# Attention and gated experts on one core: the first batch's q and k stacked on two sides of the array and turned by 64x128 transposes

## The chip, the cores and the metric

The kernel runs on one core of a Trainium2 chip. The metric is the device time of one execution in microseconds (us). The engines, as the profile names them: PE (TensorE, matrix products), PEld (its weight loads), DVE (VectorE), ACT (ScalarE), POOL (GpSimd) and SP (SyncE, which issues DMA transfers and computes nothing). Each engine works through its own list of instructions in order. Matrix products land in PSUM, eight banks of 128 x 512 words, and have to be copied out by DVE or ACT.

## What is computed

```python
B, H, S, D = 8, 8, 576, 64          # q, k, v: (B, H, S, D), float32
scores = q @ k^T / sqrt(D)
# heads 0-3: local mask, 0 <= row - col < 32
# heads 4-7: strided mask, row >= col and row % 32 == col % 32
x = softmax(masked scores) @ v       # heads side by side: (B, S, 512)

logits = x @ w_gate                  # 4 experts, the top 2 kept, softmax over these
for e in range(4):
    a = softmax(causal((x @ wq[e]) @ (x @ wk[e])^T / sqrt(64)))
    out += w_e * (a @ (x @ wv[e]) @ wo[e])
```

## The kernel before, in words

The kernel runs through eight batches. `stage1(b, hp)` does the first attention for a pair of heads (four pairs a batch: pairs 0 and 1 are local, 2 and 3 strided). It loads q and k, turns them so that the head dimension lies on partitions, forms the few scores that the mask leaves, does the softmax in six steps, multiplies by V and splits the result into a high and a low part, `xh` and `xl`, which later matmuls use three at a time to keep precision. `project` forms q and k of the experts, `values2` V and the gate, `last_scores` and `attend` the second attention, `out_tile` the output.

For batches 1 to 7 q and k are loaded in blocks and turned by VectorE (`turn`, L494). For batch 0 (`whole`) they are loaded in long rows and turned on TensorE: `tps` multiplies 64x64 blocks by an identity (L462, 200 matmuls in four quarters of the array), and `tp_out` copies each PSUM bank into the tile `qkt` (the copies stand under L304, the line of a helper). A local pair's q goes to one tile `nat` and its k to another, with both heads on partitions (128 rows of 2304 B); a strided pair's are 36 rows of 4096 B for each head. They rest in tiles that other things use later (`vs`, and `p`, the P2 rings). Scores are L535 (local) and L542 (strided), values L634 and L657, the transposes of strided softmax results L605, projections of batch 0 L794, V projections L711 and L719 (the short last tile).

V of batch 0 and 1 goes through three tiles `VR` (`load_v`, L505 local, L512 strided; two DMAs a step, one for each head), weights through `load_weights` (L388, L391). All loads are issued by SyncE.

The order is written out: `PLAN` is a list of words such as `242S0`, each an operation's number, the engine that does it and the buffer slots it takes, and `schedule` issues them in that order. An operation that is queued on an engine waits there for its data, and what stands behind it waits too. `fill` (L1022) is a matmul of ones that nobody reads; the plan places 60 of them where TensorE would stand idle.

A DMA from SyncE or ScalarE is counted on one of eight counters, and a DMA waits for the last one on its counter. In the listings below `DMAHW3` is such a counter, and `[waits DMAHW3_49]` a wait for it.

Of the kernel before, what the change touches and what calls it, by code (L numbers as in the profile page):

```python
# [20 lines left out]
def attention_moe_kernel(  # L21
# [69 lines left out]
    def op(kind, eng, n, key, fn, r=(), w=(), mode=None, npk=0, after=()):  # L91
# [24 lines left out]
        242S0 43P0 230S1 17P1 60S0 44P2 151S0 29P3 7P4 99S1 38P5 61S2 28P6 243A0 110S1 12P7 231A0 21P0 236S2 232G0  # L116
        47P1 141S0 30P2 139S1 244G0 15P3 26P4 100S3 24P5 11P6 182S0 32P7 3P0 109S 62P10 101P21 140S 237A 63D 71S2
        64P3 238G 102A 27P4 65D 66P5 183S1 184S 23P6 67A 4P7 68P0 1P1 303S4 69A 6P2 155S 16P4 74P360 152S 76D 148P70
        138S 75D 239S 78D0 13P5 149A 181S 77D 80G 37P1 34P2 144P0 79G 82A 227S3 84D 81A 103P4 245S 145D 107P6 73S
        83D 104A 10P3 108D 240A 35P5 270S0 14P1 85D 241G 20P7 112S 105P2 86G 45P0 228A 106D 8P3 271S 87G 41P4 246A  # L120
        229D 46P5 70S 247D 113P611 88D0 142P7 114D 115D 72S 146P0 116D1 143A 117D 118G 154S 0P3 147A 31P2 119G 40P4
        120A 251S0 36P5 191P61 122D 121A 123D 156P170 124D 192A 125G 185P3 111S 157D 126G 158D 33P2 334S2 159D2 186A
        39P0 160D 187P4 153S 161G 127D1 162G 163A 89P561700 188D 252A0 164A 253G0 165D 302S 166D 9P2 92A 224S 96A
        2P0 93D 94A 189P3 167D 90A 95D 150S 169G 91D 97D 128P426011 194S2 98G 190A 168G 1260P10 135A 131A 136D 129A
        170P570 132D 225A 137G 195S 130D 199P301 133A 226G 172D 171A 197S 134D 1266P2 193S 200D 173P4722 201D 202D3
        1267P 203D 204G 174A 198S 178A 48P5 175D 25P6 176A 205G 206A 179D 19P3 233S 1246P0 177D 208D 180G 207A 18P5
        272S 1247P 209D 196S 1296P61 210D 1268P 211G 300S 1253P3 266S3 1289P7 212G 1297P 234A 1254P 213P451 235D
        254S1 1261P 215A 214D 1290P 257S 1262P 216P5433 307S1 1291P 248S 221A 217A 1298P 222D 219A 255A 220D 1303P4
        218D 273S 256G 1248P 306S 1304P 258A 223G 267S 1292P 259D 301S 1305P 1294A0 1249P 268S 1293A 249A 1269P
        1295G0 335S 1250A 250D 1263P 269S 1271A1 1251A 275D0 1299P 1264A 260S0 1252G1 1281P50 1270A 1265D 1300A 337S  # L130
        1272D 1301A 341S0 1275P7 308D1 1302G 1282A 338S 304S 336S 1283P0 1255P 1276A 274D 1284A 1318P160 261A0
        1323P250 1320D0 1319D 280P700 1322A 263S1 262G0 1324D 1321A 1325D 305S 1326A 1306P 281D 339S 1327A 1273P6
        282D 312S1 1307A 283D0 340S 1308D 284G 1279P1 477S4 1274A 342D0 264A 276S0 265G 285A 309D 1256P 313S 1309P2
        1280A 286D 1257A 1277P5 1258A 377S3 343D 1259G 372S2 1310P 1278A 287D 42P7 344S2 1285D00000 288G 5P0
        1375P461 474S 1328P131 376S 1349P571 1329D 371S 1286A 1311P 1330D 373S 1331A 22P0 1376D1 346S 1332A 1350D2
        1312P 374S 1313A 1287D 1314A 1378A 311S 1316P1301 1315D 1288G 1352A 1333D 1317P40 1351D 1337G 310S 350P520
        1354D 1338G 1353A 1411D3 370S 1385P710 1335G 352D 375S 1336G 351D 407S1 1355D 1334G 277S 353D1 1339G 1356A
        1340P322 314P541 1387D 476S 354G 1342A 1386D 1341A 411S0 1380P121 1389A 1357D 279S 315D 1343P370 1358G 355A
        1382D 1381D 1360G 1388A 1361P523 356D 1362A 347S 1383A 316D 1359G 1363A 357D 408S 378D0 1345A 358G 1364P151
# [942 lines left out]
```

## Time and profile before

| what | us |
|---|---|
| median of 3 runs | 451.67 |
| lowest and highest run | 451.58, 454.35 |
| the profiled execution | 455.44 |
| its span, first to last instruction | 453.7 |

The page's busy times are for the whole span, and its slices show how an engine's share changes. PE's matmuls are pipelined, so that a busy PE need not be at its peak, and a filler is as busy as a useful matmul. The granted clock is a share of TensorE's 2.4 GHz: 1.00 is 2.4 GHz, 0.50 is 1.2 GHz. A "pass" in what follows is one MATMUL record of the trace; a float32 matmul leaves two, a transpose one.

### The profile page before, as it was taken

To read this page: it belongs to the slowest core of one execution; us is meant where nothing else is said; L and a number is where in the kernel's file an instruction comes from. 1 tells how busy PE (TensorE), PEld (TensorE's weight loads), DVE (VectorE), ACT (ScalarE), POOL (GpSimd) and SP (SyncE) were. 2 spreads that over 40 slices of the span, in tenths; PEclk is the share of its full clock that TensorE was granted. 3 is DMA by queue.
4 is the path that set the end of the run, shared out by engine and by line. 5 is a ranking of instruction groups with operands and counts; after the bars stand their busy time and mean duration, and the time that the engine had idled before them with its cause. 6 is when DMAs were issued, how large, how long until landed. Compare 5 with 4: busy or idle time off the path is not lost.

```text
span 453.7 us, 19338 instructions
## 1 busy us (share of the span) xinstructions
PE 436.0 (96%) x7878; PEld 385.8 (85%) x7878; DVE 338.5 (75%) x1037; ACT 270.6 (60%) x835; POOL 224.7 (50%) x352
## 2 busy tenths in 40 slices
PE   8899996899999999999999999999999999999995
PEld 8799995689978988789879997899889998898874
DVE  5257489997799799878789799877998297733650
ACT  2235457863776575734677474845984475755762
POOL 7145456834277715746255616581777017450550
PEclk9789999999999999999999999999999999999999
DMA  6642665555655553644553364335363330200113
GB/s 173 162 92 56 126 115 104 103 104 95 105 97 91 98 125 73 133 88 88 112 119 67 70 129 89 64 67 143 71 148 88 79 84 21 77 1 23 48 49 116
DMA packets 189817, 41.91 MB, mean 92 GB/s; under 512 B 184064, under 2 KB 184064, under 8 KB 189728
## 3 DMA queue, kind: packets, MB, share of 16 engines
q1 hardware_dynamic: 189728, 40.67, 42.7%
q8 instruction: 62, 1.02, 0.9%
q14 instruction: 27, 0.22, 0.2%
HBM read 31.20 MB, written 9.44 MB: 90 GB/s over the span
## 4 chain that ended last, share of the span: by engine, by line
PE 72%; DVE 12%; POOL 7%; issue 3%; DMA 3%; SPq 1%; ACT 1%; DVEq 0%; POOLq 0%; ACTq 0%
PE bank L783 17%; PE bank L1003 9%; PE bank L711 9%; PE bank L974 6%; PE bank L882 5%; PE bank L941 5%; POOL p L922 4%; PE bank L634 3%; PE bank L657 3%; PE bank L462 3%; PE bank L794 3%; PE bank L1022 2%; PE bank L535 2%; DVE p L889 2%; PE bank L719 2%
## 5 line engine op out<-in xcount | busy, mean ns | idle before, releaser
L922 POOL TENSOR_SCALAR p<-p,st,wt 128x256 f32<-128x256 f32 (+3 forms) x128 | 76.2, 608 | 17.6 <-DVE st L902 8.4
L894 ACT ACTIVATE p<-p,st 128x256 f32<-128x256 f32 (+3 forms) x128 | 71.4, 564 | 4.1 <-DVE st L889 3.7
L889 DVE CUSTOM_DVE_ANT_0 p<-bank,m_cau 128x256 f32<-128x256 f32 (+3 forms) x128 | 56.4, 483 | 6.2 <-PE bank L882 5.6
L494 DVE STREAM_TRANSPOSE qkt<-nat 128x576 f32<-128x576 f32 x56 | 55.7, 1006 | 5.0 <-DMA nat<-in_k_dram 4.7
L974 PE MATMUL bank<-th,vs 128*64 128x192 f32 (+4 forms) x512 | 48.0, 337 | 0.5 <-ACT th L304 0.5
L304 ACT COPY th<-bank 128x256 f32<-128x256 f32 (+2 forms) x112 | 43.2, 429 | 8.1 <-PE bank L941 7.3
L974 PEld LDWEIGHTS bank<-th,vs 128*64 128x64 f32 x512 | 33.6, 137 | 13.5 <-issue 5.9
L941 PE MATMUL bank<-ident,p 64*128 64x64 f32 x800 | 39.6, 227 | 5.7 <-POOL p L922 4.6
L941 PEld LDWEIGHTS bank<-ident,p 64*128 64x128 f32 x800 | 33.3, 138 | 13.6 <-POOL p L922 6.9
L812 POOL TENSOR_TENSOR qkl<-kf,qk 128x288 fp32r<-128x288 f32 x32 | 25.8, 806 | 35.2 <-ACT qk L803 30.2
L803 ACT CAST qk<-bank 128x288 fp32r<-128x288 f32 x64 | 25.4, 401 | 29.9 <-PE bank L783 29.8
L619 DVE TENSOR_TENSOR xl<-bank,xh 128x160 fp32r<-128x160 f32 (+3 forms) x112 | 31.1, 322 | 10.8 <-ACT xh L617 10.4
L711 PE MATMUL bank<-wh_v,xh 128*128 128x260 f32 x128 | 37.1, 290 | 0.0
L711 PE MATMUL bank<-wh_v,xl 128*128 128x260 f32 x128 | 36.3, 283 | 0.0
L711 PE MATMUL bank<-wl_v,xh 128*128 128x260 f32 x128 | 36.1, 282 | 0.0
L304 DVE COPY th<-bank 128x384 f32<-128x384 f32 (+2 forms) x48 | 23.0, 496 | 15.6 <-PE bank L941 15.3
L617 ACT CAST xh<-bank 128x160 fp32r<-128x160 f32 (+3 forms) x112 | 27.6, 323 | 11.3 <-PE bank L634 6.1
L571 POOL TENSOR_TENSOR p1s<-p1s,st 128x648 f32<-128x648 f32 (+1 forms) x18 | 20.7, 1157 | 27.2 <-DVE st L569 26.0
L783 PE MATMUL bank<-xh,wh_q 128*128 128x288 f32 x112 | 33.8, 301 | 0.0
L783 PE MATMUL bank<-xh,wh_k 128*128 128x288 f32 x112 | 33.3, 297 | 0.0
L783 PE MATMUL bank<-xl,wh_k 128*128 128x288 f32 x112 | 33.0, 294 | 0.0
L783 PE MATMUL bank<-xh,wl_k 128*128 128x288 f32 x112 | 33.0, 294 | 0.0
(158 smaller groups left out, 1274.4 us busy)
## 6 DMA issues: line engine op xcount, KB each, us to landing
out_dram<-ys SPq DMA_DIRECT2D x32, 256.0 KB
nat<-in_q_dram SPq DMA_DIRECT2D x112, 72.0 KB
nat<-in_k_dram SPq DMA_DIRECT2D x112, 72.0 KB
v<-in_v_dram SPq DMA_DIRECT2D x96, 40.0 KB
v<-in_v_dram SPq DMA_DIRECT2D x128, 22.5 KB
v<-in_v_dram SPq DMA_DIRECT2D x64, 27.0 KB
v<-in_v_dram SPq DMA_DIRECT2D x32, 48.0 KB
out_dram<-ys SPq DMA_DIRECT2D x8, 128.0 KB
```

Source lines behind the costliest of these rows:

```text
L304: (nc.scalar.copy if e == "ACT" else nc.vector.tensor_copy)(dst, src)
L494: nc.vector.transpose(dst, src)
L617: op("xh", "A", n_, key, lambda e, s_=s_, x_=x_: nc.scalar.copy(x_(xh.t), s_(xa.t)), r=[xa], w=[xh[u]])
L619: op("xl", "D", n_, key + 0.5, lambda e, s_=s_, x_=x_: nc.vector.tensor_sub(x_(xl.t), s_(xa.t), x_(f(xh.t))), r=[xa, xh[u]], w=[xl[u]])
L711: nc.tensor.matmul(vp.t[:m, :NV], xx.t[:, t0:t0 + m], ww.t[:, kt, :], start=i == 0, stop=i == 11)
L783: nc.tensor.matmul(pj.t[:, :HS], ww.t[:, kt, ep * 128:(ep + 1) * 128], xx.t[:, c], start=i == 0, stop=i == 11)
L889: lambda e, sp=sp, p=p, a=a, nk=nk, ci=ci: nc.vector.tensor_tensor_reduce(out=p.t[:, a, :nk], in0=sp[a].t[:, :nk], in1=m_cau[:, S - nk:], ...
L894: op("exp2", "A", nk, k_ + 1, lambda e, p=p, a=a, ci=ci, nk=nk: nc.scalar.activation(p.t[:, a, :nk], p.t[:, a, :nk], AF.Exp, bias=st.t[:, ...
L922: lambda e, p=p, a=a, ci=ci, t=t, nk=nk: nc.gpsimd.tensor_scalar(p.t[:, a, :nk], p.t[:, a, :nk], st.t[:, 14 + ci + a:15 + ci + a], wt.t[:, ...
L941: nc.tensor.transpose(tp[hf].t[:, 64 * c:64 * c + 64], src, ident[r, r])
L974: nc.tensor.matmul(acc.t[o, c0:c0 + cn], vw, th[a].t[:, s0:s0 + cn], start=j == 0, stop=j == idx[-1], skip_group_check=True)
L1003: nc.tensor.matmul(yp.t[:, :DM], xx.t[:, c0:c0 + 128], ww.t[:, ep, :], start=i == 0, stop=i == 5)
```

## The change

In batch 0, q of a pair now goes to partitions 0 to 63 and k to partitions 64 to 127 of the same tile, the two heads side by side in the free dimension. A 64x128 block (both heads of q, or of k) is turned by one transpose instruction (L468 in the new numbering, from here on), so that there are 100 in place of 200 matmuls. Each load now moves 256 B runs, and there are four loads for a local pair (two before) and eight for a strided one (four before). The loads of pair 2 are issued by ScalarE. The steps of `load_v` for the local pairs of batch 0 may be issued by ScalarE or GpSimd; the plan gives eight DMAs to each. V of batch 1 may not be loaded ahead of batch 0's. The plan is a new one throughout.

```diff
-        nat = [(NAT if local or not whole else (VS, P2[3])[hp % 2]).new(f"nat{x}_{n}") for x in range(2)]
+        if whole:
+            nat = [r.new(f"nat{x}_{n}") for x, r in enumerate([VS] if local else [(P2[3], VS)[hp % 2]] * 2)]
+        else:
+            nat = [NAT.new(f"nat{x}_{n}") for x in range(2)]
...
+            def load(e, z, x, src, h, g0, g1):
+                dma = nc.scalar if e == "ACT" else nc.sync
+                dst = raw(z)[64 * x:64 * x + wd, :128 * (g1 - g0)].rearrange("p (i h d) -> p i h d", h=2, d=D)
+                dma.dma_start(dst[:, :, h], src[b, h0 + h].rearrange("(p i) d -> p i d", i=nb)[:, g0:g1])
+
+            for z in range(len(nat)):
+                g0, g1 = (0, 9) if local else (8 * z, 8 * z + 8)
+                for x, src in enumerate((q, k)):
+                    for h in range(2):
+                        op("load_big", "A" if hp == 2 else "S", wd, hp, lambda e, z=z, x=x, src=src, h=h, g0=g0, g1=g1: load(
+                            e, z, x, src, h, g0, g1), w=[nat[z]], npk=wd)
...
-                            for h in range(2):
-                                r = slice(64 * h, 64 * h + wd)
-                                nc.tensor.matmul(tp.t[64 * h:64 * h + 64, wd * (g - g0):wd * (g - g0) + wd],
-                                                 raw(x)[r, D * g:D * g + D], ident[r, r], start=True, stop=True)
...
+                        for x in range(2):
+                            r = slice(64 * x, 64 * x + wd)
+                            c = 128 * (g if local else g - g0)
+                            nc.tensor.transpose(tp[x].t[:, wd * (g - g0):wd * (g - g0) + wd], raw(z)[r, c:c + 128], ident[r, r])
...
-            op("load_v", "S", 336 if local else 198, (k0 - 25 if b else 4.0 + hp), lambda e, i=i: load_v(e, i), w=[vt],
-               npk=336 if local else 198)
+            o = op("load_v", "AG" if local and not b else "S", 336 if local else 198, (k0 - 25 if b else 4.0 + hp),
+                   lambda e, i=i: load_v(e, i), w=[vt], npk=336 if local else 198, after=FIRST if b == 1 else ())
+            if b == 0:
+                FIRST.append(o)
...
-        242S0 43P0 230S1 17P1 60S0 44P2 151S0 29P3 7P4 99S1 38P5 61S2 28P6 243A0 110S1 12P7 231A0 21P0 236S2 232G0
```

TensorE before, at the start, where the first fillers end (`fz` are fillers, `nat` are q and k of the local pairs, `ident` the identity, `qkt` the turned q and k):

```order
L1022 MATMUL bank_64<-fz 128x128
L462 MATMUL bank_65<-ident,nat_176 64x64 x10
L462 MATMUL bank_66<-ident,nat_177 64x64 x10
L462 MATMUL bank_67<-ident,nat_178 64x64 x10
L1022 MATMUL bank_68<-fz 128x128
L462 MATMUL bank_69<-ident,nat_176 64x64 x8
...
L535 MATMUL bank_67<-qkt_181 32x64
```

TensorE after, at the same place (`vs_174` now holds both q and k of pair 0):

```order
L1031 MATMUL bank_65<-fz 128x128
L468 MATMUL bank_66<-ident,vs_174 128x64
L468 MATMUL bank_67<-ident,vs_174 128x64
L468 MATMUL bank_66<-ident,vs_174 128x64
L468 MATMUL bank_67<-ident,vs_174 128x64
...
L544 MATMUL bank_65<-qkt_181 32x64
```

Before, 17 fillers stand ahead of the first transpose, and q of both local pairs and k of one are turned ahead of the scores; after, 10 fillers, then the 18 transposes of pair 0 alone, 9 fillers, and its scores. Up to the first L719 (L728 after) there are 46 fillers, 200 transposes and 75 projection matmuls before, and 52, 100 and 87 after.

ScalarE before, from its first instruction (`th` holds raw weights, `wh` their high part):

```order
L394 ACT_TABLE_LOAD
L394 CAST wh_q_254<-th_170 128x256 [waits DMAHW0_49]
L394 CAST wh_k_252<-th_171 128x256 [waits DMAHW1_49]
L394 CAST wh_q_254<-th_172 128x256 [waits DMAHW1_49]
L304 COPY qkt_183<-bank_66 128x5x64 [waits DVE_49,PE_49]
L304 COPY qkt_181<-bank_69 128x4x64 [waits DVE_49,PE_49]
```

ScalarE after, at the same place (`p_166` and `p_167` take q and k of pair 2, `v_189` and `v_185` V of the local pairs):

```order
L450 DMA p_166<-in_k_dram 36x8x64
L450 DMA p_167<-in_q_dram 36x8x64
L450 DMA p_167<-in_k_dram 36x8x64 x2
L450 DMA p_167<-in_q_dram 36x8x64 [waits DMAHW0_49]
L450 DMA p_166<-in_q_dram 36x8x64 [waits DMAHW2_49]
L512 DMA v_189<-in_v_dram 32x6x64 [waits DMAHW4_49,DVE_49]
L512 DMA v_189<-in_v_dram 32x6x64 [waits DMAHW6_49]
L512 DMA v_185<-in_v_dram 32x6x64 [waits DMAHW0_49]
L512 DMA v_185<-in_v_dram 32x6x64 [waits DMAHW2_49]
L304 ACT_TABLE_LOAD
L304 COPY qkt_181<-bank_69 128x4x64 [waits PE_49]
L394 CAST wh_q_254<-th_170 128x256 [waits DMAHW3_49]
```

Ten loads have moved ahead of the table load and of the first copy; six more stand behind the next copy.

GpSimd after, behind its masks, before the first step of the softmax (before, no load stands on GpSimd):

```order
L512 DMA v_185<-in_v_dram 32x5x64
L321 AFFINE_SELECT m_str<-m_str 64x54
L512 DMA v_185<-in_v_dram 32x5x64
L321 AFFINE_SELECT m_str<-m_str 64x54
L321 AFFINE_SELECT m_loc<-m_loc 32x64
L512 DMA v_189<-in_v_dram 32x5x64 x4
L512 DMA v_185<-in_v_dram 32x5x64 x2
L580 TENSOR_TENSOR p1l_80<-p1l_80,st_199 128x320 x2
```

Eight loads stand ahead of the subtraction of pair 0 (L580, which was L571).

## Rows read from the trace of the kernel before

**Rows 1.** The page: busy us, share of the span and instructions of each engine

```profile
PE 436.0 (96%) x7878; PEld 385.8 (85%) x7878; DVE 338.5 (75%) x1037; ACT 270.6 (60%) x835; POOL 224.7 (50%) x352
```

**Rows 2.** Busy time by stretch: stretch, length, each engine (instructions), PEclk, DMA share, GB/s

```profile
0.00:6.25 6.25, 4.58 (x21) 4.59 (x22) 4.78 (x36) 2.09 (x3) 4.43 (x16) 1.00 0.47 121
6.25:16.50 10.25, 8.12 (x209) 7.28 (x209) 3.15 (x6) 2.10 (x4) 5.47 (x13) 1.00 0.82 205
16.50:26.70 10.20, 10.20 (x124) 9.45 (x121) 3.00 (x8) 2.82 (x7) 2.32 (x4) 0.50 0.57 131
...
60.00:100.00 40.00, 35.08 (x795) 28.44 (x790) 37.89 (x108) 29.09 (x90) 26.02 (x37) 1.00 0.53 96
```

**Rows 3.** Chain of waits, 0 to 60 us: start, us, what

```profile
9.70 6.22 DMA vs<-in_k_dram
...
19.07 3.82 PE bank L462 x68
22.89 2.00 PE bank L1022 x8
...
27.43 0.90 PE bank L535 x58
28.33 1.99 PE bank L462 x64
30.32 1.09 PE bank L1022 x8
...
35.78 1.08 PE bank L634 x62
...
40.23 0.52 PE bank L605 x12
40.75 0.84 PE bank L542 x44
...
42.18 0.83 PE bank L657 x44
...
44.88 2.77 PE bank L794 x21
...
55.24 1.02 PE bank L719 x8
```

**Rows 4.** Groups by line and shape, the transposes of batch 0: busy us, mean ns

```profile
L462 PE MATMUL bank<-ident,nat 64*64 64x64 f32 x144 | 6.6, 255 | 0.0
...
L462 PE MATMUL bank<-ident,vs 36*64 36x36 f32 x128 | 5.5, 251 | 2.1 <-DMA vs<-in_k_dram 2.1
...
L462 PE MATMUL bank<-ident,p 36*64 36x36 f32 x128 | 4.6, 224 | 0.0
```

**Rows 5.** Instructions of TensorE in order of time, the first: start, us

```profile
1.67 6.23 PE L1022 MATMUL bank<-fz 128*128 128x128 f32 x34 [1.67 <-DVE fz L312]
```

**Rows 6.** Waits of SyncE's queue up to 60 us: us in total, times, longest

```profile
SPq L512 <- PE bank L634: 4.5, 1, 4.5
...
SPq L451 <- DMA vs<-in_q_dram: 0.8, 1, 0.8
SPq L451 <- DMA nat<-in_k_dram: 0.7, 1, 0.7
```

**Rows 7.** Instructions in order of time, start to 27 us

```profile
0.79 1.28 ACT L394 ACT_TABLE_LOAD   x1 [0.79 <-PEq L1066]
0.80 0.45 SPq L388 DMA_DIRECT2D th<-in_moe_wq_dram  x1
...
3.15 0.41 ACT L394 CAST wh_q<-th 128x256 fp32r<-128x256 f32 x1 [1.07 <-DMA th<-in_moe_wq_dram]
...
26.18 1.07 SPq L391 DMA_DIRECT2D p<-in_moe_w_gate_dram  x1
```

**Rows 8.** DMA queue 1 from 6 to 8 and from 20.5 to 22.5 us: packets, MB, share of 16 engines

```profile
q1 hardware_dynamic: 563, 0.60, 94.4%
...
q1 hardware_dynamic: 1727, 0.37, 87.4%
```

More of the change, by code (lines that the diff above doesn't have):

```diff
@@ L270, in attention_moe_kernel @@
+        2579D 2628P422 2599A 2623G 2600A 2648G 2631P173 2630D 2629A 2601P3 2633A 2632D 2634P600 2604A 2602A 2605D
+        2603D 2649P500 2635A 2652P421 2651D 2650A 2636D 2655P71 2654A 2653A 2663P32 2657D 2656A 2666P51 2664A 2665S
+        2658P0 2667A 2668S 2669P20 2659A 2661A 2660D 2662D 2672P62 2670A 2671S 2675P41 2673A 2674S 2676A 2677S
     """
@@ L453, in stage1 @@
-            for g0, g1 in zip(cuts, cuts[1:]):
-                for x in range(2):
-                    tp = RB.new(f"tp{g0}{x}_{n}")
-                    cn = wd * (g1 - g0)
-                    def tps(e, tp=tp, g0=g0, g1=g1, x=x):
-                        for g in range(g0, g1):
-                            for h in range(2):
-                                r = slice(64 * h, 64 * h + wd)
-                                nc.tensor.matmul(tp.t[64 * h:64 * h + 64, wd * (g - g0):wd * (g - g0) + wd],
-                                                 raw(x)[r, D * g:D * g + D], ident[r, r], start=True, stop=True)
-                    def out(e, tp=tp, g0=g0, g1=g1, x=x, cn=cn):
-                        if local:
-                            copy(e, at(qkt.t, 0, 128, x * S + g0, [[1, g1 - g0], [nb, wd]]),
-                                 tp.t[:, :cn].rearrange("p (i t) -> p i t", t=wd))
-                        else:
-                            copy(e, at(qkt.t, 0, 128, x * S + NJ * g0, [[NJ, g1 - g0], [1, NJ], [16 * NJ, 2]]),
-                                 tp.t[:, :cn].rearrange("p (i u a) -> p i u a", u=NJ, a=2))
-                    op("tp", "P", 2 * (g1 - g0), k0 - 14 + 0.1 * g0, tps, r=[nat[x]], w=[tp, qkt[x]], mode=MQ)
-                    op("tp_out", "AD", cn, k0 - 13 + 0.1 * g0, out, r=[tp], w=[qkt[x]])
@@ new lines, in stage1, with raw @@
+            nb, wd, cuts = (9, 64, (0, 5, 9)) if local else (16, 36, (0, 8, 16))
+            def raw(z):
+                return nat[z].t.rearrange("p a c -> p (a c)")
+            def load(e, z, x, src, h, g0, g1):
[8 more added lines that the diff above has]
+                            e, z, x, src, h, g0, g1), w=[nat[z]], npk=wd)
@@ new lines, in stage1, with tps, out @@
+            for g0, g1 in zip(cuts, cuts[1:]):
+                tp = [RB.new(f"tp{g0}{x}_{n}") for x in range(2)]
+                cn = wd * (g1 - g0)
+                z = 0 if local else g0 // 8
+                def tps(e, tp=tp, g0=g0, g1=g1, z=z):
+                    for g in range(g0, g1):
+                        for x in range(2):
+                            r = slice(64 * x, 64 * x + wd)
+                            c = 128 * (g if local else g - g0)
+                            nc.tensor.transpose(tp[x].t[:, wd * (g - g0):wd * (g - g0) + wd], raw(z)[r, c:c + 128], ident[r, r])
+                def out(e, tp=tp, g0=g0, g1=g1, x=0, cn=cn):
+                    if local:
+                        copy(e, at(qkt.t, 0, 128, x * S + g0, [[1, g1 - g0], [nb, wd]]),
+                             tp[x].t[:, :cn].rearrange("p (i t) -> p i t", t=wd))
+                    else:
+                        copy(e, at(qkt.t, 0, 128, x * S + NJ * g0, [[NJ, g1 - g0], [1, NJ], [16 * NJ, 2]]),
+                             tp[x].t[:, :cn].rearrange("p (i u a) -> p i u a", u=NJ, a=2))
+                op("tp", "P", g1 - g0, k0 - 14 + 0.1 * g0, tps, r=[nat[z]], w=[*tp, qkt[0], qkt[1]], mode=MR)
+                for x in range(2):
+                    op("tp_out", "AD", cn, k0 - 13 + 0.1 * g0, lambda e, out=out, x=x: out(e, x=x), r=[tp[x]], w=[qkt[x]])
```

322 lines of the change are left out of this document (155 added, 167 removed).

## The prediction

> **What bounds the kernel now.** I began with the engine totals and the busy time by stretch. TensorE is busy for 436.0 of the 453.7 us span, VectorE for 338.5 [rows 1]. The stretches say that this is not one limit: between 60 and 100 us VectorE is busy for 37.89 of 40 us, and before 26.7 us every engine but TensorE has room, while the granted clock of TensorE goes from 1.00 (2.4 GHz) to 0.50 (1.2 GHz) between 16.5 and 26.7 us [rows 2]. Then I read the chain of waits over the first 60 us [rows 3]. Up to about 56 us it is nearly all TensorE, but much of that is filler matmuls (L1022, of no use to the output) and the transposes of batch 0 (L462). The reader is to see that filler is planned waiting: where it stands in the chain, what really limits is the arrival of q and k, the copies out of PSUM, or the softmax. One real wait for data stands in the chain: 6.22 us from the issue of a k load to its first transpose at about 16 us.
>
> I call the first matmul of L719 (the short last tile of the V projection of batch 0) the mark. Before, it starts at 55.24 us [rows 3]. The change rewrites what comes ahead of the mark; behind it the same instructions run in another order. So I sum TensorE up to the mark.
>
> **Prices at 2.4 GHz, from [rows 3].** A filler is two passes: 8 passes in 1.09 us, 0.136 each. A 64x64 transpose by matmul is also two passes: 64 in 1.99 us, 0.031 each; the 200 of batch 0 are 144 + 128 + 128 = 400 passes [rows 4]. For the new 64x128 transpose the nearest row is L605, also 64 rows by 128 columns: 12 in 0.52 us, 0.043 each, one pass. A block of local scores is 0.90 us, of strided scores 0.84, of local values 1.08, of strided values 0.83; a projection matmul 2.77 / 21 = 0.132.
>
> **Before, up to the mark.** The first fillers end at 1.67 + 6.23 = 7.9 us [rows 5], the last one lapping over the first transpose: 7.8. The other 58 filler passes are 7.9 us, 400 transpose passes 12.4, two blocks of each of the four kinds 7.3, the 24 transposes of L605 1.0, 75 projections 9.9. Sum 46.3 us. The mark is at 55.24, so 8.9 us are not in it: the wait at 16 us, the half clock (below), switches between shapes.
>
> **After, up to the mark.** Ten fillers stand ahead of the first transposes, not 17. At the 6.23 us / 34 of the old ones they end near 5.3 us. The four loads of pair 0 need not be there yet: the first load of the kernel is issued at 0.80 us and used at 3.15 us, 2.35 later [rows 7], the fourth is issued some 1.4 us behind the first, and the 2304 packets of pair 0 share the DMA engines with the 1152 of the first four loads on ScalarE. Small packets cost 0.874 x 2 us x 16 / 1727 = 16.2 ns of one engine [rows 8], so 3456 of them take 3.5 us from about 2.4 us on. I take 6.7 us (5.3 to 7.8). Then 42 fillers, 84 passes, 11.4 us; 100 transposes 4.3 us (from 3.1, the price of the narrow one, to 8.0, two passes at 0.04); the same 7.3 and 1.0; 87 projections 11.5. Sum 42.2 us, against 46.3: 4.1 less. Twelve projections more lie ahead of the mark, 1.6 us that no longer follow. At equal work the start is **5.7 us** shorter, if the 8.9 us outside the sum stay as they are. That is the step on which the forecast rests.
>
> **The loads.** All q and k of batch 0 (2.36 MB) now come as 9216 packets of 256 B: 9216 x 16.2 ns / 16 = 9.3 us of all 16 engines. In a stretch with many long packets they moved 0.60 MB in 2 us at a share of 94.4%, 318 GB/s at a full share [rows 8], 7.4 us for the same bytes. So 1.9 us more of transfer. The DMA share is 0.82 between 6.25 and 16.5 us and 0.47 and 0.57 beside it [rows 2], so most of this is hidden, and it shows only if pair 1 or 2 arrives late. SyncE loses 16 issues of V and 4 of q and k of pair 2 and gains 8 for the other pairs: 12 fewer at 0.45 us [rows 7], 5.4 us earlier for the weights and batch 1. It also waited 4.5 us with V of pair 3 for the values of a local pair [rows 6]; that wait stays, since the buffers are still three, and comes as early as those values do.
>
> **ScalarE, the new wait.** Ten loads now stand ahead of its table load, which was free at 0.79 us, and of its first copies. Each load waits until an earlier one on the same of eight counters has landed; ScalarE uses four of them, so its fifth load waits for its first and its ninth for its fifth. Such waits were 0.7 and 0.8 us on SyncE [rows 6]. Two rounds of 2.35 us from 0.80 on put the ninth at 5.5 us; if the rounds take 3.5 us, since all share the engines, at 7.8. Two issues of 0.45 and 1.28 us of table load follow: the first copy starts between 7.7 and 10 us, the second ends some 1.7 us later with a weight cast between. The scores of pair 0 wait for it: between 9.4 and 11.7 us, while TensorE by the sum is there at 6.7 + 0.8 + 2.4 = 9.9. So 0 to 1.8 us late; I take 1, inside the 8.9. Behind the last four V loads are queued the copies of pair 1 and the first exponentials.
>
> **GpSimd** issues the other eight loads of the local V, ahead of its first subtraction. No row shows a load issued there. Bounds: SyncE's 0.45 us for one and 1.07, its longest single row here [rows 7]; 3.6 to 8.6 us. GpSimd was busy for 4.43 + 5.47 = 9.9 us by 16.5 us [rows 2], some 1.4 of it the subtraction, so it is free at 12 to 17 us, where the softmax of pair 0 wants it near 14. I take the low end, as the same kind of instruction, and keep 3 us for the range. The Trainium skill, "DMA: Bandwidth & Descriptors", section "Latency and other measured facts", gives about 1 us for the first byte on this path, spent on writing descriptors; by it the eight would be 8 us, near the upper end. No run here shows it yet.
>
> **The clock.** In the half-clock stretch 8 filler passes took 2.00 us, not 1.09, and 68 transpose passes 3.82, 0.056 each [rows 3]. TensorE was idle for 2.1 us in the stretch ahead of it [rows 2]. The new order has such a place too, at the first scores. I leave the loss as it was.
>
> **The rest.** The same instructions; batch 0's attention to 100 us is VectorE's. Batch 1 must arrive 5.7 us sooner, and SyncE's 5.4 us allow that. A new order may be worth 2 us either way.
>
> The profiled execution took 455.44 us, its span 453.7 plus 1.74; the median of the runs is 451.67. The sum is a difference, 5.7 us, and I take it from the median: 451.67 - 5.7 = **446.0 us**.
>
> **Rivals.**
> 1. The loss shrinks as well: no wait at 16 us and no half clock. Of the 8.9 us go the 2.1 that TensorE is idle between 6.25 and 16.5 us [rows 2] and 4.8 of the half clock (rival 4): 446.0 - 6.9 = 439.1. For it: fewer loads on SyncE ahead of pair 1. Against it: busier DMA engines.
> 2. The start is bound by arrival and by ScalarE's queue, not by TensorE. Then what the transposes lose is spent waiting, and the mark stays at 55 to 57: **451.7 us**, no change. For it: idle where filler stands, and the waits above. Against it: two queues and 12 fewer issues on SyncE.
> 3. The gain is given back behind the mark. VectorE, at 95% from 60 to 100 us, needs batch 1's data and the scores; if it can't start sooner, also 451.7. Against it: it is fed by the same chain.
> 4. Slower: the clock stays at 1.2 GHz until the first projection. It has risen once the fillers had run for some 4.5 us; the new ones are fewer and a pause follows. Price: 66 filler passes at 0.114 more, 7.5; 100 transposes at 80% more, 3.4; 4.8 us of scores and values likewise, 3.9; sum 14.8, less the 4.8 that a like count gives for the old half-clock stretch (20 filler passes and 100 transpose passes). So 446.0 + 10.0 = 456.0 us, above before if over 5.7 of the 10 come true. It is decided at the end of the first fillers. The Trainium skill, "TensorE: Matmul & The Clock Gate", section "Part 4: PE-mode transpose", says that transpose mode does not count as busy as a matmul does; the change turns 200 matmuls into 100 such transposes, so by it this rival gains. The old rows neither bear it out nor refute it, as the transposes there stand between matmuls.
> 5. The change does what it says: the order shows 100 transposes at the start. Only half of V's loads on other engines are on ScalarE.
>
> **How the numbers follow.** Forecast 0.40, rival 1 0.18, rival 2 0.20, rival 3 0.09, rival 4 0.13. One per cent, 4.5 us, is about what a measurement of this kernel tells from no change. Over 1% faster (below 447.2) are two thirds of the forecast's chance (a spread of 3 us), rival 1 and a little of 2: 0.50. Over 1% slower (above 456.2) is half of rival 4 and a rest for the order behind: 0.12. Within 1%: 0.38. The range runs from rival 1, and 0.6 us below it, to rival 4: 438.5 to 456.0. The forecast alone is 443 to 449.
>
> **What would show it.** Right: the first transpose near 6.5 us, 100 passes of about 0.045 us, first scores at 10 to 12, the mark near 51, and 453.7 - 55.2 - 1.6 = 397 us behind it. Rival 1: the mark below 47 and the clock at 1.00. Rival 2: the mark at 55 with long idle on TensorE. Rival 3: the mark at 51, but over 400 us behind it, with TensorE idle for VectorE. Rival 4: clock 0.50 beyond 26.7 us. Most at risk are the wait for pair 0 and ScalarE's queue.

## The result, and the profile after

The changed kernel took 449.6 us (median of 16 runs, 445.89 to 453.19) where the kernel before took 454.38 (16 runs, 450.42 to 456.54): a ratio of 0.9896, 95% interval 0.9861 to 0.993, which is 4.7 us (3.2 to 6.3). The forecast was 5.7 us. The time itself lies 3.6 us above the 446.0 on record, 2.7 of them because the base does: 451.67 over three runs then, 454.38 over sixteen now. Ratios here and below leave out the executions that stood well above the rest of their kernel, among them the traced ones of E1 (586.51 us, at a mean granted clock of 0.655) and of E4 (456.92, 0.978). The profiled execution took 447.38 us, its span is 445.7, 8.0 below the profiled one of before; the two lie at different places of their spreads.

The page's engine totals of the changed kernel, which answer to [rows 1], show TensorE with 6.7 us less to do and as full as before:

```profile
PE 429.3 (96%) x7582; PEld 379.4 (85%) x7582; DVE 341.1 (77%) x1049; ACT 267.5 (60%) x827; POOL 226.0 (51%) x356
```

Its busy time by stretch, for [rows 2] (the columns are the same):

```profile
0.00:6.25 6.25, 4.57 (x20) 4.34 (x20) 4.78 (x36) 0.00 (x0) 4.42 (x16) 1.00 0.73 161
6.25:16.50 10.25, 8.81 (x149) 8.11 (x149) 4.13 (x10) 3.97 (x7) 7.49 (x17) 1.00 0.94 188
16.50:26.70 10.20, 8.61 (x270) 7.73 (x270) 8.88 (x24) 5.47 (x16) 5.88 (x10) 1.00 0.62 132
26.70:40.00 13.30, 13.26 (x267) 12.22 (x266) 8.70 (x25) 6.36 (x19) 7.71 (x13) 0.87 0.60 121
60.00:100.00 40.00, 35.00 (x808) 28.77 (x814) 35.88 (x107) 26.26 (x83) 24.85 (x37) 0.96 0.50 90
```

The stretch from 16.5 to 26.7 us stood at a clock of 0.50 before and stands at 1.00 now. The 1.00 ahead of it is not to be trusted: where no clock record lies the view prints full speed, and the pace of the fillers below says 1.2 GHz. The DMA share in the second stretch rose from 0.82 to 0.94.

The chain of waits from 0 to 60 us, for [rows 3]:

```profile
2.90 4.66 DMA vs<-in_q_dram
7.69 1.34 PE bank L468 x18
9.03 4.14 PE bank L1031 x18
13.17 1.15 PE bank L544 x68
...
15.02 1.27 PE bank L468 x34
...
17.38 0.62 PE bank L468 x16
...
19.23 3.75 DMA th<-in_moe_wq_dram
...
49.80 0.96 PE bank L728 x8
```

The mark is at 49.80 us in place of 55.24: 5.4 us. By the instructions' own start it is 49.55, against 55.08; these starts are used below. Behind it are 396.1 us, against 398.6. So in this pair of traces the gain stands at the start, as forecast. How it came about there is another matter. Instructions in order of time, changed kernel:

```profile
1.68 4.64 PE L1031 MATMUL bank<-fz 128*128 128x128 f32 x20 [1.68 <-DVE fz L312]
7.69 1.34 PE L468 MATMUL bank<-ident,vs 64*128 64x64 f32 x18 [1.38 <-DMA vs<-in_q_dram]
8.35 1.28 ACT L304 ACT_TABLE_LOAD   x1 [8.35 <-DMA v<-in_v_dram]
8.96 4.21 PE L1031 MATMUL bank<-fz 128*128 128x128 f32 x18
9.64 0.61 ACT L304 COPY qkt<-bank 128x256 f32<-128x256 f32 x1
10.09 3.42 POOL L512 DMA_DIRECT2D v<-in_v_dram  x6
10.36 0.74 ACT L304 COPY qkt<-bank 128x320 f32<-128x320 f32 x1
13.10 1.22 PE L544 MATMUL bank<-qkt 64*32 64x64 f32 x72
15.02 0.46 PE L468 MATMUL bank<-ident,vs 64*128 64x64 f32 x8
15.84 0.72 POOL L580 TENSOR_TENSOR p1l<-p1l,st 128x320 f32<-128x320 f32 x1 [2.34 <-DVE st L578]
```

And the same place before:

```profile
12.87 0.97 PE L535 MATMUL bank<-qkt 64*32 64x64 f32 x72
15.97 1.31 PE L462 MATMUL bank<-ident,vs 36*64 36x36 f32 x28 [2.12 <-DMA vs<-in_k_dram]
```

The reader is to see two things. First, the scores of pair 0 end at 14.3 us now and ended at 13.8 before, though TensorE had less to do by then. By the prediction's prices it had 46 filler passes, 92 transpose passes and the scores before, 10.0 us, and has 38, 18 and the scores now, 6.8. These 3.2 us are spent: the first transposes wait 1.38 us for q, and 18 filler passes take 4.21 us, 0.23 each, where 2.4 GHz would make them 2.45. Second, all of the lead is won behind that point: 41.2 us from the end of these scores to the mark before, 35.2 now. Of the 6.0 us, 2.0 are work (46 filler and 308 transpose passes before; 66, 82 and twelve more projections now). The other 4.0, by subtraction, are the pause of 2.12 us and the half clock behind it, less what the new order has of both. The two stretches, before and changed, tell these apart:

```profile
13.84:55.08 41.24, 39.12 (x871) 36.38 (x870) 22.11 (x58) 15.90 (x46) 16.07 (x26) 0.88 0.50 102
14.32:49.55 35.23, 33.35 (x675) 30.61 (x676) 24.75 (x63) 17.70 (x53) 16.18 (x25) 0.95 0.63 126
```

TensorE idles for 2.1 us of the one and for 1.9 of the other: the pause is gone, but several small ones have come. The clock takes 0.12 x 41.2 = 4.9 us of the one and 0.05 x 35.2 = 1.8 of the other, some 3 less. So most of the 4.0 is the clock.

### The profile page after: what moved, and what is told of

Same layout as the page of the kernel before. It is cut to its first block, busy times and chain, and to the rows that moved or that the text cites. A ratio compares the mean times of both kernels' runs of the same rounds, so it can differ in the third digit from the quotient of the medians.

```text
span 445.7 us, 18764 instructions
## 1 busy us (share of the span) xinstructions
PE 429.3 (96%) x7582; PEld 379.4 (85%) x7582; DVE 341.1 (77%) x1049; ACT 267.5 (60%) x827; POOL 226.0 (51%) x356
## 4 chain that ended last, share of the span: by engine, by line
PE 86%; DVE 4%; DMA 4%; POOL 2%; SPq 2%; issue 1%; ACT 1%; POOLq 0%; ACTq 0%
PE bank L792 19%; PE bank L1012 12%; PE bank L720 10%; PE bank L983 10%; PE bank L891 7%; PE bank L950 6%; PE bank L643 4%; PE bank L666 3%; PE bank L803 3%; PE bank L544 3%; PE bank L1031 3%; PE bank L551 2%; PE bank L848 2%; PE bank L614 2%; PE bank L728 2%; POOL p L931 1%
## 5 line engine op out<-in xcount | busy, mean ns | idle before, releaser
L931 POOL TENSOR_SCALAR p<-p,st,wt 128x128 f32<-128x128 f32 (+3 forms) x128 | 76.2, 608 | 25.2 <-DVE st L911 14.9
L903 ACT ACTIVATE p<-p,st 128x384 f32<-128x384 f32 (+3 forms) x128 | 71.3, 561 | 7.4 <-DVE st L898 7.3
L898 DVE CUSTOM_DVE_ANT_0 p<-bank,m_cau 128x512 f32<-128x512 f32 (+3 forms) x128 | 56.7, 482 | 0.7 <-PE bank L891 0.3
L304 ACT COPY th<-bank 128x256 f32<-128x256 f32 (+2 forms) x108 | 41.7, 427 | 7.7 <-PE bank L950 6.9
L628 DVE TENSOR_TENSOR xl<-bank,xh 128x270 fp32r<-128x270 f32 (+3 forms) x112 | 30.9, 322 | 9.2 <-ACT xh L626 9.0
L580 POOL TENSOR_TENSOR p1s<-p1s,st 128x648 f32<-128x648 f32 (+1 forms) x18 | 20.7, 1157 | 32.3 <-DVE st L578 28.9
L792 PE MATMUL bank<-xl,wh_q 128*128 128x288 f32 x112 | 33.0, 294 | 0.0
## 6 DMA issues: line engine op xcount, KB each, us to landing
v<-in_v_dram SPq DMA_DIRECT2D x128, 22.5 KB
```

The source lines that it names most:

```text
L304: (nc.scalar.copy if e == "ACT" else nc.vector.tensor_copy)(dst, src)
L628: op("xl", "D", n_, key + 0.5, lambda e, s_=s_, x_=x_: nc.vector.tensor_sub(x_(xl.t), s_(xa.t), x_(f(xh.t))), r=[xa, xh[u]], w=[xl[u]])
L792: nc.tensor.matmul(pj.t[:, :HS], ww.t[:, kt, ep * 128:(ep + 1) * 128], xx.t[:, c], start=i == 0, stop=i == 11)
L898: lambda e, sp=sp, p=p, a=a, nk=nk, ci=ci: nc.vector.tensor_tensor_reduce(out=p.t[:, a, :nk], in0=sp[a].t[:, :nk], in1=m_cau[:, S - nk:], ...
L903: op("exp2", "A", nk, k_ + 1, lambda e, p=p, a=a, ci=ci, nk=nk: nc.scalar.activation(p.t[:, a, :nk], p.t[:, a, :nk], AF.Exp, bias=st.t[:, ...
L931: lambda e, p=p, a=a, ci=ci, t=t, nk=nk: nc.gpsimd.tensor_scalar(p.t[:, a, :nk], p.t[:, a, :nk], st.t[:, 14 + ci + a:15 + ci + a], wt.t[:, ...
```

## The experiments

Ratios are to the kernel before, on the same chip and in the same series, with their 95% intervals; 1% is 4.55 us. Mark and first scores are from one profiled run each; those of E4, E12 and E14 took 0.6 to 1% more than their medians, that of E1b 0.6% less. E1 has none that can be used.

| kernel | ratio | first scores, us | mark, us |
|---|---|---|---|
| before | 1 | 12.87 | 55.08 |
| changed | 0.9896 (0.9861 to 0.993) | 13.10 | 49.55 |
| changed, again | 0.9897 (0.9817 to 0.9977) | 12.85 | 48.27 |
| E1, turns as matmuls | 1.0068 (1.0028 to 1.0108) | | |
| E1b, the same again | 1.0115 (1.0033 to 1.0197) | 13.50 | 54.89 |
| E14, each transpose twice | 0.9936 (0.9901 to 0.9971) | 11.75 | 54.48 |
| E3, V on SyncE | 0.9967 (0.9946 to 0.9989) | 11.77 | 55.50 |
| E6, pair 2 on SyncE | 0.9959 (0.9936 to 0.9983) | 11.79 | 52.95 |
| E4, four more fillers | 0.9933 (0.9902 to 0.9964) | 11.84 | 52.43 |
| E9, pair 1 loaded first | 0.9886 (0.982 to 0.9953) | 12.07 | 51.62 |
| E10, E4, E9 and an early table load | 1.0047 (1.0014 to 1.008) | 14.84 | 53.52 |
| E8, before, fillers moved to the pause | 0.993 (0.9888 to 0.9971) | 12.44 | 50.99 |
| E13, before, fillers added in the pause | 0.9987 (0.9958 to 1.0016) | 12.43 | 50.10 |
| E12, before, fewer first fillers | 0.9978 (0.9952 to 1.0004) | 12.56 | 55.06 |

**The changed kernel again**, beside E8, E9 and E10.

> The changed kernel unchanged, as the yardstick on this chip for the kernels beside it. Its ratio to the kernel before was 0.9896 (0.9861 to 0.993) on another chip; by every theory the same within 0.5%: 0.985 to 0.995.

0.9897, as on the first chip. Its mark is 1.3 us earlier than in the first trace (no half clock between 26.7 and 40 us), its span 1.9 us longer. So a mark in one trace is good to a microsecond or two, and says less of the end than that.

**E1, E1b and E14: the turns made longer.** E1 undoes the transposes alone, E14 doubles them.

```diff
-nc.tensor.transpose(tp[x].t[...], raw(z)[r, c:c + 128], ident[r, r])
+nc.tensor.matmul(tp[x].t[...], raw(z)[r, c:c + 128], ident[r, r], start=True, stop=True)   # E1
+for _ in range(2): nc.tensor.transpose(tp[x].t[...], raw(z)[r, c:c + 128], ident[r, r])   # E14
```

> Undoes one part: the 100 turns of a 64x128 block are matmuls by the identity (two passes each) in place of transposes (one pass), so 100 more passes ahead of the mark, in the new order, with the new loads. Theory A (TensorE's work ahead of the mark sets the start): at the 0.039 us of a pass at full clock the mark moves from 49.55 by 3.9 us, less what the 1.4 us wait for the first copies and other idle places take up, so 2 to 4 us, to 51.5 to 53.5, and the time goes from 449.6 to 451.5 to 453.5. Rival B (loads, copies and the softmax set the start, TensorE's passes lie in waits): the mark stays within 1 us and the time within 1 us of 449.6. Rival C (the clock: matmuls count as busy where transposes do not): the clock is up before the 14 us of the changed kernel, and the mark is no later than 49.6.

> The 100 turns as matmuls of two passes again, for a trace of an undisturbed run beside its time: the first one measured 1.0068 (1.0028 to 1.0108) of the kernel before, 1.7% or 7.8 us over the changed kernel, twice what 100 passes at 0.04 us are. Theory F (work and pauses, and the clock that falls behind pauses): the first scores end 1.3 to 2.6 us later than in the changed kernel (18 passes more, at half the clock), the copies of pair 1 and the softmax move with them, and half-clock stretches of 3 to 10 us stand on work that counts before the mark, at 55 to 58. Theory A (passes alone): the mark at 52 to 53.5, and the rest of the 7.8 us behind it. Time by both 1.000 to 1.011 of the kernel before.

> The changed kernel with each of the 100 transposes issued twice into the same place: 100 passes more, as in the run with two passes, but all of them transposes. Theory A and F (passes count, not their kind): the same time as the run with two passes, within 0.6%. Rival K (transposes leave the clock low where matmuls raise it): the clock rises later or falls sooner than in the run with two passes, and the time is 1% or more above it. Rival L (a second transpose of the same data costs nothing much): within 0.4% of the changed kernel, 0.986 to 0.994.

Measured: with 100 transposes more the time rises by 0.4% (1.8 us; the interval of E14 reaches from no loss to 3.4), with the turns as matmuls by 1.7 and 2.2% (8 to 10 us). The expectations priced every pass more at 0.039 us, whatever its kind, and so came to 4 us for both. TensorE's busy time on the turns (L468) up to 60 us, with their number, in the changed kernel, E14 and E1b (the columns are length, PE, PEld, PEclk, DMA share, GB/s):

```profile
0.00:60.00 60.00, 4.61 (x100) 4.10 (x100) 0.97 0.72 141
0.00:60.00 60.00, 8.69 (x200) 8.22 (x200) 0.91 0.70 135
0.00:60.00 60.00, 12.09 (x200) 11.62 (x200) 0.94 0.71 134
```

E14 adds 4.1 us of it and loses 1.8; E1b adds 7.5 and loses 10, E1 8. Turns of the first pair and of a later one, with the stretch around the later one, in E1b and in E14:

```profile
7.41 2.33 PE L468 MATMUL bank<-ident,vs 64*128 64x64 f32 x36 [1.10 <-DMA vs<-in_q_dram]
...
28.77 3.77 PE L468 MATMUL bank<-ident,vs 36*128 36x36 f32 x64
28.00:32.00 4.00, 4.00 (x66) 3.88 (x65) 3.50 (x11) 1.55 (x4) 3.03 (x6) 1.00 0.45 88
```

```profile
7.58 1.45 PE L468 MATMUL bank<-ident,vs 64*128 64x64 f32 x36 [1.64 <-DMA vs<-in_q_dram]
...
28.06 3.63 PE L468 MATMUL bank<-ident,vs 36*128 36x36 f32 x64
28.00:32.00 4.00, 4.00 (x67) 3.87 (x66) 0.92 (x2) 0.99 (x2) 0.88 (x3) 0.50 0.50 98
```

The 64 passes near 28 us take 0.059 us each in E1b at a clock of 1.00, and 0.057 in E14 at 0.50. At 1.00 the transposes of this shape take 0.037 (32 in 1.19 us, E14 at 18.23 us). So a matmul pass of this shape is longer than a transpose at the same clock, and a matmul turn takes two. The loss of E1 and E1b is of the size of the work that they add: TensorE's work at the start does count, and with matmuls for its turns the new order is slower than the kernel before (1.0068 and 1.0115).

The clock goes with it, and how much of the loss is the clock's is not told apart. Its mean is 0.971 to 0.985 over the runs of E1 and E1b that count, 0.984 to 0.996 in nine of E14's ten. The two traces hide this (0.982 and 0.984): that of E14 is one of its longest, and so the marks are alike. The rival by which transposes leave the clock low is not borne out, since 200 of them went with the higher clock. Why matmuls went with the lower one these runs don't show.

**E3 and E6: the loads back on SyncE.** E3 gives SyncE the local V, E6 the loads of pair 2, by the letter of the word alone.

```diff
-71G0 111A2 72A 110G 109G 70G 112A 73A
+71S0 111S2 72S 110S 109S 70S 112S 73S
```

```diff
-141A0 142A1 145A 144A 143A 139A 138A 140A
+141S0 142S1 145S 144S 143S 139S 138S 140S
```

> Undoes one part: all 16 loads of the local V of batch 0 are issued by SyncE again, at the same places of the order; ScalarE and GpSimd issue none. ScalarE's table load then waits for no V load and runs near 5 us in place of 8.35, so the first copies go as soon as the first transposes have ended (9.0). Theory A (TensorE's work sets the start): first scores at 12.5 to 13 in place of 13.1 us, since 18 filler passes stand between at half the clock, the mark within 1 us, the time within 1 us of 449.6 or up to 2 us longer where SyncE, with 16 issues of 0.6 us more (10 us), brings pair 2's or the weights' loads late. Rival B (ScalarE's queue sets the start): first scores at 11.5 or before, the mark 1.3 us or more earlier. Rival D (V's move off SyncE is what the gain comes from): the mark 3 to 6 us later, back at 53 to 55, with TensorE or ScalarE waiting for loads of SyncE.

> Undoes one part: the eight loads of pair 2 are issued by SyncE, at the same places of the order, and ScalarE keeps only its eight loads of V. SyncE issues eight more at 0.6 us each, 4.8 us, most of them ahead of pair 0's later loads. Theory A (first transposes wait for pair 0, whose loads now stand behind others in one queue): first transposes at 9 to 11 us in place of 7.7, and the mark later by the part of that which fillers do not hide, 1 to 3 us; time 450.5 to 452.5. Rival E (a second queue is worth nothing, since the DMA engines are the limit): first transposes within 0.5 us of 7.7 and the mark within 1 us.

E3 loses 0.7% and E6 0.6% (3.2 and 2.9 us) against the changed kernel's 0.9896. Neither went the way that was written for theory A: the first scores come 1.3 us sooner in both, and the loss stands behind them. TensorE of E3 in order of time:

```profile
15.39 0.46 PE L468 MATMUL bank<-ident,vs 64*128 64x64 f32 x8 [2.01 <-DMA vs<-in_q_dram]
...
24.16 1.51 PE L643 MATMUL bank<-pt,v 32*64 32x64 f32 x84 [2.29 <-DVE pt L604]
...
30.17 0.49 PE L1031 MATMUL bank<-fz 128*128 128x128 f32 x2 [2.16 <-DVE p1s L567]
```

Three pauses of 2 us, at pair 1's q and then in the softmax, whose ScalarE waits for weights that come behind V (4.8 us for `th`). E6 in order of time, and its stretch:

```profile
10.94 0.71 PE L1031 MATMUL bank<-fz 128*128 128x128 f32 x4 [2.11 <-ACT qkt L304]
...
17.21 0.78 PE L468 MATMUL bank<-ident,vs 64*128 64x64 f32 x8 [3.19 <-DMA vs<-in_q_dram]
```

```profile
16.50:26.70 10.20, 9.49 (x152) 8.81 (x156) 5.91 (x13) 4.63 (x11) 3.05 (x5) 0.53 0.70 149
```

Pair 1's q is awaited for 3.19 us and the clock is 0.53 from 16.5 to 26.7 us; it had fallen near 13 us, behind the pause of 2.11. Both kernels have a lower mean clock than the changed one over the runs that count: 0.973 to 0.984 in E3, 0.976 to 0.988 in E6, 0.981 to 0.995 there. So rival D, that V's move carries gain, is borne out for E3, and rival E is refuted: each of the two groups of loads is worth some 3 us, its waits and the clock behind them together. That is less than the turns of E1; against E14 the intervals overlap.

**E4: four more first fillers.**

```diff
-139A 53P0 156S1 71G0 111A2 17P1 100S
+139A 53P0 156S1 71G0 111A2 17P1 2678P4 2679P5 2680P6 2681P7 100S
```

> Four more fillers (8 passes) behind the ten first ones, so that TensorE has no pause of 1.4 us ahead of the first transposes; nothing else differs. Rival C (the clock is what the start lost): the granted clock is at 2.4 GHz from about 7 us on in place of 14, the 18 filler passes behind the first transposes take 2.4 us in place of 4.2, first scores at 11.5 to 12 in place of 13.1, the mark 1 to 2 us earlier (47.5 to 48.5) and the time 448 to 449. Theory A in its bare form (work, not clock): 4 fillers at 0.23 are 1.9 us of which 1.4 lie in the pause; the mark stays within 0.5 us, or is 0.5 later. Rival B (copies and loads): first scores within 0.3 us of 13.1.

The clock rose early and the scores came at 11.84 us, as rival C had it; the mark came 2.9 us later, as nobody had it, and the time is 0.4% longer (intervals overlap). E4 in order of time, and its stretch:

```profile
8.34 1.83 PE L1031 MATMUL bank<-fz 128*128 128x128 f32 x14
...
15.82 0.69 PE L468 MATMUL bank<-ident,vs 64*128 64x64 f32 x8 [2.38 <-DMA vs<-in_q_dram]
```

```profile
16.50:26.70 10.20, 10.20 (x209) 9.34 (x211) 6.17 (x14) 5.08 (x11) 3.67 (x5) 0.54 0.60 129
```

Pair 1's q is there at 15.8 us, whatever TensorE does before. The changed kernel's slow fillers ahead of its scores thus cost nothing that E4 could win back: they fill the wait for that load. What E4 saves there comes back, in this trace, as a pause of 2.38 us with 1.2 GHz behind it, the picture of the kernel before. The traced execution is E4's longest. Two of its others had a mean clock of 0.996, a loss of 1.8 us, where this stretch alone loses 4.7; so they can't have had it whole, and the 2.9 us at the mark are not those of every run.

**E9 and E10: pair 1's loads earlier.** E9 puts them ahead of weights and V on SyncE and the first weight cast behind the second copy; E10 adds E4's fillers and a one-column copy on ScalarE that takes the table load forward.

```diff
-25P3 102S1 141A0 ... 243S0 142A1 20P5 145A 240S ... 101S ... 156S1 ... 100S ... 99S
+25P3 102S1 101S 100S 99S 141A0 ... 243S0 142A1 20P5 145A 240S ... 156S1
-244A0 11P1 306S0 66A
+11P1 306S0 66A 244A0
```

> The changed kernel with the three later loads of pair 1 ahead of two loads of weights and of V on SyncE, and the first weight cast of ScalarE behind the second copy. Theory G (up to 15 us the start waits for the loads of pair 1, which SyncE issues only at 7.6, 10.0 and 11 us): pair 1 is there by 11 to 12 us in place of 15, but the first scores end at 14.3, so the transposes of pair 1 move ahead by what pause there was, under 1 us, and the mark by 0 to 1.5 us; time 448 to 450. Theory A (TensorE's work sets the start from 7.7 on): the same mark within 0.5 us. Rival H (weights come late by the swap): ScalarE waits for a cast near 11 us, the first scores come after 13.5, and the mark is 1 us or more later.

> The same order of loads, four more fillers ahead of the first transposes, and a copy of one column on ScalarE behind its fourth load, so that its table load stands there and not ahead of the first copy of q and k. Theory G with the clock: the clock is up near 6 us, the first scores come at 10.5 to 11.5 in place of 13.1 and, since pair 1 is there by then, no pause of over 0.5 us follows and no half-clock stretch; the mark at 45.5 to 47.5 and the time 446 to 447.5, 2 to 4 us below the changed kernel. Rival I (the clock falls some 10 us after it has risen whatever TensorE does, as in the kernel before and in the run with more fillers alone): half clock from about 16 to 26 us, the mark at 49 to 51, the time that of the changed kernel or up to 2 us longer.

E9 in order of time:

```profile
12.70 0.76 ACT L394 CAST wh_q<-th 128x256 fp32r<-128x256 f32 x2 [1.51 <-DMA th<-in_moe_wq_dram]
...
14.06 3.99 ACTq L512 DMA_DIRECT2D v<-in_v_dram  x4
...
18.09 1.11 ACT L304 COPY qkt<-bank 128x256 f32<-128x256 f32 x2 [4.64 <-DMA v<-in_v_dram]
...
18.76 1.22 PE L1031 MATMUL bank<-fz 128*128 128x128 f32 x4 [3.23 <-ACT qkt L304]
```

Pair 1 is turned at 13.6 us, 1.4 sooner, and its copies wait in ScalarE's queue behind a late weight and four V loads: rival H, in another place than was written. The ratio is that of the changed kernel all the same (0.9886), with a mark 2 to 3 us later. E10 is slower than the kernel before. Its first transposes wait until 10.60 us: pair 0's last load takes 7.57 us from its issue, 4.49 in E9. From 4 to 6 us the core moved 148 GB/s, 254 in E9, with the same loads ahead. Whether the table load beside them does that was not tried alone.

**E8, E13 and E12: the kernel before and its pause.** The pause of 2.12 us stands behind the scores of pair 0. E8 moves seven first fillers into it, E13 puts seven new ones there, E12 cuts the seven first ones to one column.

```diff
-47P1 141S0 30P2 139S1 244G0 15P3 26P4 100S3 24P5 11P6 182S0 32P7 3P0 109S
+47P1 141S0 139S1 244G0 100S3 182S0 109S
-74P360 152S
+74P360 30P1 15P2 26P1 24P2 11P1 32P2 3P1 152S   # E8
+74P360 2674P1 2675P2 2676P1 2677P2 2678P1 2679P2 2680P1 152S   # E13, first fillers as before
```

> The kernel before, with seven of its 17 first fillers moved into the pause of 2.1 us behind the scores of pair 0. Work, loads and their order are the kernel before's. Theory F, formed on the runs so far (half of the gain is the half-clock stretch, which the kernel before had at 16.5 to 26.7 us on work that counts and the changed kernel spends on fillers before 14 us): with the pause filled, and the clock risen later, the half-clock stretch behind 16 us shrinks or moves ahead of it, the mark comes at 50.5 to 53.5 in place of 55.24, and the time 2 to 5 us below the kernel before's. Theory A in its bare form (the gain is TensorE's smaller work alone): the work is the same, so the mark stays within 1 us of 55.2 and the time within 1 us of the kernel before.

> The kernel before with all of its 17 first fillers and seven more in the pause behind the scores of pair 0. Theory P (the fall follows the pause): the clock rises near 6.6 us as before, no half-clock stretch of more than 3.5 us stands before the mark, which comes at 50.5 to 52.5; time 0.990 to 0.995 of the kernel before. Theory Q (the fall follows the early rise): half clock from about 16.8 to 27 us all the same, mark at 55 to 56.5, time 0.998 to 1.004.

> The kernel before, with seven of its 17 first fillers cut to one column and nothing put into the pause behind the scores of pair 0. It tells apart why the run with the filled pause gained 0.7%. Theory P (a pause of 2 us or more at 2.4 GHz is what the fall follows): the pause is still there, 2 us or more, and a half-clock stretch of 7 to 14 us follows it; mark at 54 to 56.5, time 0.997 to 1.004 of the kernel before. Theory Q (the early rise is what the fall follows, some 10 us later whatever stands between): the rise comes 1 us later, the fall as much later or not at all, mark at 50.5 to 53, time 0.990 to 0.995.

The stretch from 16.5 to 26.7 us of E8, of E13 and of E12:

```profile
16.50:26.70 10.20, 10.20 (x277) 9.52 (x274) 6.16 (x14) 4.38 (x10) 3.20 (x5) 1.00 0.63 136
```

```profile
16.50:26.70 10.20, 10.20 (x278) 9.45 (x276) 6.90 (x16) 4.90 (x11) 3.49 (x5) 1.00 0.57 125
```

```profile
16.50:26.70 10.20, 10.20 (x131) 9.49 (x128) 2.61 (x7) 2.82 (x7) 2.13 (x3) 0.53 0.58 135
```

On the clock theory P has it: with the pause filled no half clock stands here, and the mark comes at 51.0 and 50.1 us; with the pause left (2.57 us in E12) half clock and mark are as before. Not one transpose was changed for that. But of the 4 to 5 us at the mark little reached the end: 3.2 us in E8 (1.3 to 5.1), 0.6 in E13 (1.9 less to 0.7 more). E13 in two later stretches, and the kernel before at the first one's distance from its mark:

```profile
55.10:75.00 19.90, 15.80 (x258) 13.43 (x258) 18.78 (x60) 12.95 (x42) 12.40 (x19) 1.00 0.61 114
75.00:85.00 10.00, 9.72 (x221) 7.28 (x221) 9.56 (x28) 8.57 (x28) 8.94 (x13) 0.83 0.60 105
60.08:79.98 19.90, 16.30 (x268) 13.95 (x268) 19.27 (x60) 13.50 (x44) 12.94 (x19) 1.00 0.54 98
```

TensorE idles for 4.1 us between 55.1 and 75, where VectorE is at 94%; the kernel before idles for 3.6 there, so only 0.5 is new. Right behind, from 75 to 85 us, the clock falls to 0.83, which the kernel before did not have [rows 2]. By the trace 2.7 us more lie behind the mark than before (401.3 against 398.6). That is rival 3's outcome in the old order, with the clock in it as well as VectorE; what each took is not shown.

## Why the prediction was right, and where it was not

**Size and place** came out: 5.7 us forecast at the start, 5.4 in the chain, the mark at 49.8 where 51 was written, 396.1 us behind it where 397 was, 4.7 us in the times. The sum to the mark was 42.2 us; at the measured 0.039 us of a transpose (16 in 0.62; 0.043 was taken) it is 41.8, so 8.0 us lie outside it, against 8.9. That work counts is shown by E1: with the turns as matmuls TensorE has 7.5 us more to do and the time is 8 to 10 us longer.

**The step that failed** is the one named as the forecast's rest: a start shorter by the work saved, "if the 8.9 us outside the sum stay as they are". The amount stayed, its content did not. Up to the end of the first scores nothing of the 3.2 us saved shows: pair 1's load at 15 to 16 us binds there (E4), which is rival 2. Behind them 2.0 us are work and 4.0 are, in the main, the half clock that is shorter (some 3 of them), which is part of rival 1 and which the prediction left as it was. E8 and E13 take 4 to 5 us off the mark without touching the work. The two departures about cancel, 3.2 us lost and 4.0 won; that the number was hit is luck to that extent.

**"Behind it the same instructions"** held in one trace and not as a rule. E13 brings the old order to the mark at 50.1 and gains 0.6 us; E3 brings the new order there at 55.5, later than before, and still gains 1.5 (0.5 to 2.5). So the new order is worth something behind the mark, within the 2 us either way that was allowed. One difference shows in the waits of TensorE from 55 to 430 us, changed kernel and then before (us in total, times, longest):

```profile
PE bank L950 <- POOL p L931: 2.9, 5, 1.5
```

```profile
PE bank L941 <- POOL p L922: 4.6, 8, 1.4
```

With 1.5 from E3, some 3 of the 4.7 us are left for a mark 5.5 to 6.8 us earlier. This split is an estimate; its parts come from different chips and are uncertain by 1 us and more.

**The loads were mis-sized.** The 1.9 us more of transfer were rightly called hidden, but the move of issues off SyncE was given no price at the start, only time for weights and batch 1. It is worth 3.2 us for V (E3) and 2.9 for pair 2 (E6), since pair 1's q and the weights stood behind these issues; the clock behind the waits is in these figures.

**ScalarE's queue** was right: first copy at 9.64 (7.7 to 10), the second's end at 11.1. The first scores, 13.10 and not 9.4 to 11.7, were late by the fillers' half clock instead. A wait not foreseen, 3.56 us of ScalarE for `th` ahead of pair 1's exponentials, stands in the chain at 19.23; it was not tried alone.

**GpSimd**: its eight loads took 0.80, 0.60 and 3.42 us, 4.8 in all (3.6 taken, 8.6 the upper end), and it waited 2.34 us more for VectorE, so they cost nothing. The Trainium skill, "DMA: Bandwidth & Descriptors", section "Latency and other measured facts", gives about 1 us to the first byte of such a load, spent on writing descriptors; the engine was busy for 0.57 to 0.80 us with each here, and when the first byte came no row shows.

**First transposes** came at 7.69 us, near the end of 5.3 to 7.8: pair 0's last load took 4.66 us from its issue.

**Rival 4** was half true: 1.2 GHz lasted to about 14 us, and its price was nought, since fillers and a wait lay there. The Trainium skill, "TensorE: Matmul & The Clock Gate", section "Part 4: PE-mode transpose", says that transpose mode does not count as busy as a matmul does; the mean clock of E14 (0.984 to 0.996) against that of E1 and E1b (0.971 to 0.985) shows no such loss, rather the reverse.

## What to carry to other kernels

Before crediting a shorter start to less work, fill its pauses with dummy work in the old kernel: if the stretch shortens as much, the pause and the clock behind it were the cost. Undo the work alone in the new kernel as well, and read there what one piece of it takes: here two matmul passes for a transpose were not 0.04 us more but 0.08. A lead at a mark in the middle is not a lead at the end until a run shows it; try the old order with the lead and the new order without. Look for loads at the head of one queue that others wait behind; taking two groups of them to other queues was worth some 3 us each here, and the prediction had given that no price.

## What was not expected of the hardware

Slow fillers were free and fast ones were not: with the clock up at 7 us (E4, its traced run) TensorE came to a 2.4 us pause at 2.4 GHz and then ran at 0.54 of it from 16.5 to 26.7 us. Pauses of 2.1 to 3.2 us had such a stretch behind them in five kernels (before, E4, E6, E9, E12), the filled ones (E8, E13) not. E3's later two, of 2.3 and 2.2 us, had one too, and E10's two, of 3.8 and 2.8 us, a shorter one each (0.83 in both of its stretches from 6.25 to 26.7 us). The rule is not whole: E3's pause of 2.0 us at 13.4 us had none for 9 us, and E14 met half clock near 26 us behind pauses of 0.6 and 0.7.

A float32 matmul pass by the identity over a 36x128 block took 0.059 us at a clock of 1.00 (E1b), a transpose pass over the same block 0.037 (E14).

Loads of the same 256 B runs moved at 254 and at 148 GB/s in the same 2 us of two kernels (E9, E10).
